# An early order laid out anew, clamps and state transposes on other engines, four sums at the end, and other tile widths in a chunk scan with two feed-forward layers

## The chip, the cores and the metric

One core of a Trainium2 chip runs the whole program. The metric is the device time of one execution in microseconds (us). A core has TensorE (PE in the rows; its weight loads are PEld), VectorE (DVE), ScalarE (ACT), GpSimd (POOL) and SyncE (SP), each with an instruction queue of its own that is worked in order; data comes and goes by DMA transfers that SyncE or ScalarE issue (SPq, ACTq). SBUF is the on-chip memory, PSUM the eight banks into which TensorE writes.

## What is computed

Three layers follow each other. Cut to what matters:

```
x (4, 8, 768, 32)  a (4, 8, 768)  B, C (4, 8, 768, 16)           float32
for each chunk of the sequence, per batch and head:
    L    = exp(cum_i - cum_j) for i >= j      # cum: running sum of log a
    y    = ((C B^T) * L) x + (C state) * exp(cum)
    state = exp(sum log a) * state + sum_j exp(cum_end - cum_j) B_j x_j
X  = y as (3072 tokens, 256)
X1 = (silu(X w_gate) * (X w_val)) w_out       # 256 -> 1536 -> 256
out = relu(X1 w_in)^2 w_out2                  # 256 -> 2048 -> 256
```

The five weights come in double precision (64 bits), x, a, B and C in single precision.

## The kernel before

**Arithmetic.** A wide product is made from three passes of TensorE: each operand is split into a high part (`hi`, `xh_all`) and a low rest (`lo`, `xl_all`), and hi*hi, hi*lo and lo*hi are summed. A pass has 128 rows of weights and up to 512 columns of tokens.

**Weights.** A `Unit` brings two pieces of 512 KB of 64-bit weights into one of two `raw` buffers and turns them into numbers: on ScalarE `share` (L415) and `mag` (L409), the sign on ScalarE (`signs`, L420) or VectorE (`sign`, L424), `clamp` (L430) on VectorE or GpSimd, `shift` (L434) on VectorE; then `split` makes `hi` on ScalarE (L440) and `lo` on GpSimd or VectorE (L444). Nine units hold the first layer: six named gv (gate and value columns for 256 of the 1536 hidden rows, two blocks f of 128) and three named o (the way back). Eight hold the second. `engs` has four digits per unit: sign on ScalarE, clamp on GpSimd, lo on GpSimd, and whether the decode goes in two halves.

**Chunks.** 28 chunks of 112 tokens (96 the last of a batch) carry the scan. For the seven early ones (batch 0) TensorE transposes B and C (`trb`, L497), spreads the decays over the partitions (`ab`, L583) and makes the scores (`cb`, L642); VectorE scans (L592) and multiplies (`times`, L675); TensorE makes the outputs and the state (`ys`, L689); ScalarE keeps the high part (L709) and VectorE the low (L712). The state for the next chunk is turned on VectorE (L724) and put in place by four copies (L729). Later chunks get their transposes by DMA.

**GLU.** Per tile of tokens and block f: six passes for g and six for v (both L737, "front"), silu on ScalarE (L801), the product on VectorE (L804), its high part on ScalarE (L819), its low part p on GpSimd (L824), and six passes back into the sums `acc` (L851). The first 768 tokens form two tiles, 336 and 432 wide, cut into `cells` (pair of blocks, first and last chunk, exact or not) that start as weights and chunks arrive; an exact cell uses single-precision passes on `xf` and needs no splitting. The 2304 tokens after that form five tiles (`tiles`), each with 12 blocks: 60 late steps.

**Second layer.** Six tiles of 512 tokens, 16 blocks each: front L737 (`h`), relu L903, square L906, split L909 and L913, back L923; the last tile's back (L934) has its tokens as rows, 12 passes of 256 columns per block, drained by L982 and L984 and stored.

**Order.** The program is recorded as a graph of operations with costs, priorities and buffers; `Graph.order` plays them through per engine, always the operation with the lowest priority number that is ready, and the list it makes is the order in which each engine runs. The priorities come from the table `PLAN` at the end: `unit_at`, `split_at` and `chunk_at` for weights and early chunks, the order of `cells`, `pace` for late chunks, `second` for the second layer's weights. Where the plan has a gap on TensorE, idle matmuls on zeros (L227, `fills`) are put ahead of the next pass, up to `warm` nanoseconds.

Of the kernel before, what the change touches and what calls it, by code (L numbers as in the profile page):

```python
# [8 lines left out]
F32 = mybir.dt.float32  # L9
# [18 lines left out]
class Op:  # L28
    def __init__(self, eng, cost, fn, deps, prio, bufs, lat):
        self.port = False  # L30
# [5 lines left out]
class Graph:  # L36
# [14 lines left out]
    def order(self):  # L51
# [11 lines left out]
        seq = 0  # L63
        while left:
            started = True
            while started:
                started = False
                for eng, ops in avail.items():
# [20 lines left out]
                    for b in best.bufs:  # L89
                        if not b.taken:  # L90
                            b.taken = True
                            best.after.append(free[b.pool].pop(0))
                    best.start, best.took = now, best.cost
# [13 lines left out]
            while events and events[0][0] <= now:  # L107
                _, _, kind, op = heapq.heappop(events)
                if kind == 0:
                    busy[op.eng] = None  # L110
                    left -= 1
# [18 lines left out]
def kernel(  # L130
# [188 lines left out]
    op_pick = g.add("POOL", 280, setup_pick, prio=-999)  # L319
    op_eye = g.add("POOL", 300, setup_pool, [op_mt], prio=-999.5)  # L320
    op_delta = g.add("POOL", 1200, setup_delta, [op_mt], prio=-999)
    op_mask = g.add("POOL", 950, setup_mask, prio=-997)
# [3 lines left out]
    def dma(eng, n, cost, move, fn, deps=(), prio=0.0, bufs=()):  # L326

        i = g.add(eng, n * cost, fn, deps, prio, bufs, lat=0)
        o = g.add("DMA", move, None, [i], prio, bufs, lat=1700)
        o.issue = i  # L330
# [3 lines left out]
    ld_a = [dma(q, 2, 450, 200, lambda u=u: load_a(u), [], -950) for u, q in enumerate(["SP", "ACT"])]  # L334
    op_clip = g.add("DVE", 900, clip, [*ld_a, op_zero], -950)

    def keep_decays(b):
# [5 lines left out]
        b: dma("SP", 1, 450, 400, lambda b=b: keep_decays(b), [op_clip], 300 + b)  # L343
# [6 lines left out]
    class Unit:  # L350
# [3 lines left out]
        def __init__(self, srcs, prio, after=(), homes=("w", "w"), engs=("DVE", "DVE", False)):  # L354
            raw, self.v, self.hi, self.lo = Buf("raw"), Buf("w"), Buf(homes[0]), Buf(homes[1])
            deps = [
                dma("SP", 1, 450, 1650, lambda s=s, src=src: self.load(raw, s, src), after, prio, [raw])
# [95 lines left out]
    def chunk_ops(k, prio, after=(), load_after=()):  # L453
# [27 lines left out]
        if early:  # L481
# [9 lines left out]
            lb = dma("SP", 1, 480, 650, lambda: load_b(0, B), [op_eb[k % NEB], *load_after], ldp, [e])  # L491
            lc = dma("SP", 1, 480, 650, lambda: load_b(1, C), [op_eb[k % NEB], *load_after], ldp, [e])
# [20 lines left out]
            c.tr = g.add("ACT", 1480, copy_c, [o1, op_mask], prio, [psb, c.bt])  # L513
            c.ebuf = e
        else:
# [10 lines left out]
            lb = c.load = dma("SP", 2, 480, 1300, load_b, [op_bc, *load_after], ldp, [e])  # L526
# [37 lines left out]
            c.tr = dma("SP", 1, 480, 2900, transpose, [o], prio - 3, [bcs, c.bt])  # L564

        lx = dma("SP", 1, 480, 750, load_x, [*load_after, free_x], ldp, [xb])
# [34 lines left out]
        else:  # L601
# [17 lines left out]
            o = dma("SP", 1, 480, 1650, load_ab, [*load_after, kept[b]], ldp, [ab])  # L619
# [532 lines left out]
```

## Time and profile before

| | |
|---|---|
| median of 3 runs | 656.24 us |
| lowest, highest | 656.18, 659.64 us |
| the profiled execution, its own time | 658.71 us |
| span of its records | 656.5 us |
| mean granted TensorE clock in it | 0.987 of full speed |
| TensorE busy | 637.8 us |
| VectorE busy | 393.1 us |
| ScalarE busy | 339.1 us |
| GpSimd busy | 228.5 us |

The rows come from one profiled execution, so sums are set against its span of 656.5 us, with 2.2 us around it. Busy time of TensorE counts every record from start to end; matmuls overlap, and idle matmuls count too, so it is not the same as useful work.

### The profile page before, as it was taken

Reading aid. Unit: us, or ns where it says so; the run is one execution under the profiler, and the core shown is the slowest. Engines: PE = TensorE matmul, PEld = TensorE weight load, DVE = VectorE, ACT = ScalarE, POOL = GpSimd, SP = SyncE. Lnnn points to the kernel's source line nnn. Section 1 sums busy time; section 2 is a strip of 40 time slices with the busy share of each in tenths; the row PEclk is TensorE's granted clock in tenths of the full one; section 3 lists DMA queues with packets and bytes.
Section 4 is the critical chain, followed back from the end, with each engine's and each line's share of the span. In section 5 each row is a group of like instructions: output and inputs, shape, how many; then the busy total and the mean of one; then the engine's idle time right before and its main releaser. Section 6 shows DMA issues by size and latency. Waiting matters only on the chain.

```text
span 656.5 us, 9776 instructions
## 1 busy us (share of the span) xinstructions
PE 637.8 (97%) x3735; PEld 545.7 (83%) x3735; DVE 393.1 (60%) x600; ACT 339.1 (52%) x603; POOL 228.5 (35%) x225
## 2 busy tenths in 40 slices
PE   9899889999999999999999999999999999999997
PEld 7688769888887888878999988888888888888896
DVE  6689575676767647676335755555555555555543
ACT  5579777353435444455446644444444444444442
POOL 6456996654536364534654750000000000000000
PEclk9599999999999999999999999999999999999999
DMA  8488973576455656272322200010010010100100
GB/s 185 102 192 183 182 187 79 108 130 135 88 112 109 117 100 129 55 173 100 108 70 64 65 1 0 1 32 2 0 33 1 0 33 0 33 0 1 33 1 32
DMA packets 153470, 48.89 MB, mean 74 GB/s; under 512 B 141520, under 2 KB 142032, under 8 KB 153424
## 3 DMA queue, kind: packets, MB, share of 16 engines
q1 hardware_dynamic: 152880, 47.92, 34.1%
q8 instruction: 29, 0.48, 0.3%
q10 hardware_dynamic: 544, 0.36, 0.2%
q14 instruction: 17, 0.14, 0.1%
HBM read 34.03 MB, written 3.22 MB: 57 GB/s over the span
## 4 chain that ended last, share of the span: by engine, by line
PE 56%; DVE 1%; POOL 0%; ACT 0%; issue 0%; ACTq 0%
PE h L737 20%; PE acc L923 17%; PE acc L851 5%; PE v L737 5%; PE g L737 5%; PE acc L934 3%; DVE mt L675 0%; DVE L L614 0%; DVE xa L729 0%; PE ys L689 0%; POOL p L824 0%; ACT p L819 0%; DVE xl_all L712 0%; DVE t L804 0%; PE cb L651 0%
## 5 line engine op out<-in xcount | busy, mean ns | idle before, releaser
L824 POOL TENSOR_TENSOR p<-t,p 128x464 fp32r<-128x464 f32 (+3 forms) x84 | 105.4, 1260 | 112.1 <-ACT p L819 112.0
L851 PE MATMUL acc<-p,hi 128*128 128x464 f32 (+4 forms) x336 | 99.9, 374 | 8.2 <-POOL p L824 8.2
L913 DVE TENSOR_TENSOR p<-t,p 128x512 fp32r<-128x512 f32 x96 | 66.3, 690 | 67.9 <-ACT p L909 67.9
L909 ACT ACTIVATE p<-t 128x512 fp32r<-128x512 f32 x96 | 60.8, 633 | 77.9 <-PE acc L923 52.9
L906 DVE TENSOR_TENSOR t<-t 128x512 f32<-128x512 f32 x96 | 66.9, 697 | 53.8 <-ACT t L903 53.8
L923 PE MATMUL acc<-p,hi 128*128 128x512 f32 x320 | 98.5, 389 | 0.0
L804 DVE TENSOR_TENSOR t<-t,v 128x464 f32<-128x464 f32 (+4 forms) x84 | 50.3, 601 | 80.2 <-PE v L737 56.6
L819 ACT ACTIVATE p<-t 128x464 fp32r<-128x464 f32 (+4 forms) x84 | 48.0, 572 | 91.8 <-DVE t L804 83.9
L903 ACT ACTIVATE t<-h 128x512 f32<-128x512 f32 x96 | 57.5, 599 | 63.1 <-PE h L737 62.9
L851 PEld LDWEIGHTS acc<-p,hi 128*128 128x128 f32 x336 | 62.1, 191 | 17.8 <-POOL p L824 12.0
L737 PE MATMUL h<-xh_all,hi 128*128 128x512 f32 x192 | 74.9, 390 | 0.0
L737 PE MATMUL h<-xl_all,hi 128*128 128x512 f32 x192 | 74.9, 390 | 0.0
L737 PE MATMUL h<-xh_all,lo 128*128 128x512 f32 x192 | 74.7, 389 | 0.0
L923 PEld LDWEIGHTS acc<-p,hi 128*128 128x128 f32 x320 | 60.1, 188 | 12.4
L801 ACT ACTIVATE t<-g 128x464 f32<-128x464 f32 (+5 forms) x86 | 44.9, 524 | 42.5 <-PE g L737 39.5
L737 PE MATMUL g<-xh_all,lo 128*128 128x464 f32 (+4 forms) x168 | 60.8, 362 | 1.5 <-POOL lo L444 1.4
L923 PE MATMUL acc<-p,lo 128*128 128x512 f32 x160 | 62.2, 389 | 0.0
L737 PE MATMUL g<-xh_all,hi 128*128 128x464 f32 (+4 forms) x168 | 61.2, 364 | 0.0
L851 PE MATMUL acc<-p,lo 128*128 128x464 f32 (+4 forms) x168 | 61.1, 364 | 0.0
L737 PE MATMUL v<-xh_all,hi 128*128 128x464 f32 (+4 forms) x168 | 60.6, 361 | 0.0
L737 PE MATMUL v<-xh_all,lo 128*128 128x464 f32 (+4 forms) x168 | 60.6, 361 | 0.0
L737 PE MATMUL v<-xl_all,hi 128*128 128x464 f32 (+4 forms) x168 | 60.5, 360 | 0.0
(101 smaller groups left out, 1128.4 us busy)
## 6 DMA issues: line engine op xcount, KB each, us to landing
ab<-decay SPq DMA_DIRECT2D x21, 452.0 KB, 4.0
raw<-in_moe_w_out_dram SPq DMA_DIRECT2D x14, 512.0 KB, 4.7
raw<-in_moe_w_in_dram SPq DMA_DIRECT2D x8, 512.0 KB, 3.9
raw<-in_moe_w_gate_dram SPq DMA_DIRECT2D x6, 512.0 KB, 3.9
raw<-in_moe_w_val_dram SPq DMA_DIRECT2D x6, 512.0 KB, 5.2
xa<-in_x_dram SPq DMA_DIRECT2D x24, 112.0 KB, 2.9
out_dram<-o SPq DMA_DIRECT2D x40, 64.0 KB, 1.9
bc<-in_B_dram SPq DMA_DIRECT2D x18, 56.0 KB, 3.0
```

The lines of the kernel that those rows point to most:

```text
L737: nc.tensor.matmul(ps, l, r, start=(i == 0), stop=(i == len(terms) - 1))
L801: nc.scalar.activation(t[:, :n], gg(), AF.Silu)
L804: nc.vector.tensor_tensor(tb.t[:, :n], tb.t[:, :n], vv(), op=ALU.mult)
L819: nc.scalar.activation(p[:, 0, :n], tb.t[:, :n], AF.Copy)
L824: e.tensor_tensor(p[:, 1, :n], tb.t[:, :n], p[:, 0, :n].bitcast(F32), op=ALU.subtract)
L851: nc.tensor.matmul(ps, l, r, start=bank not in done_f, stop=f == NF - 1, skip_group_check=True,)
L903: nc.scalar.activation(new(tb, [P, TN], F32, "t"), ph.t, AF.Relu)
L906: nc.vector.tensor_tensor(tb.t, tb.t, tb.t, op=ALU.mult)
L909: nc.scalar.activation(new(pb, [P, 2, TN], F32R, "p")[:, 0, :], tb.t, AF.Copy)
L913: e.tensor_tensor(pb.t[:, 1, :], tb.t, pb.t[:, 0, :].bitcast(F32), op=ALU.subtract)
L923: nc.tensor.matmul(acc[-1 - i][m], l.t[:, w], pb.t[:, r, :], start=(f == 0 and s == 0), stop=(f == NF2 - 1 and s == 2),)
L934: nc.tensor.matmul(ps, pb.t[:, l, tk], r, start=(f == 0 and s == 0 and q % 2 == 0), stop=(f == NF2 - 1 and s == 2), skip_group_check=True,)
```

## The change

1. *The planner.* Transfers in the plan are served in the order in which they became ready instead of by priority; no more than 2600 pieces may be queued; several costs are other numbers. These act on the order alone.
2. *The early order.* New numbers for `chunk_at`, `unit_at`, `split_at`, `cells`, `pace` and `second`. The nine units now come as gv2, o1, gv3, o2, gv5, gv4, gv1, gv0, o0. The exact cell is two chunks (224 columns) of unit gv2 instead of one of unit gv4, and a cell of one chunk (112 columns) stands beside it. The second layer's weights are asked for later.
3. *Engines of the decode* (`engs`). No clamp of the first layer is on GpSimd (before: seven of nine units, 12 instructions); signs on ScalarE for seven units (before all nine); lo on GpSimd for four units (before four others) and halves for three (before five): the digits stand in the diff, in the order gv0, o0, gv1, gv2, o1, gv3, gv4, o2, gv5.
4. *Early states.* ScalarE copies the state, TensorE transposes it in two passes (`turn`), ScalarE puts it in place. Late chunks keep VectorE.
5. *Last tile.* Its sums lie in four banks instead of two, and the last block's back is four operations, each with its own drain and store.
6. *Tiles* of 256 and four of 512 tokens instead of three of 464 and two of 456.
7. *`rest`.* The low half of p is made on VectorE in the first 17 late steps, then on GpSimd; in the cells it stays on GpSimd.
8. *Fillers.* Every planned gap of TensorE over 150 ns gets two idle matmuls more than its length gives.

The diff, cut to its core:

```diff
                     for op in ops:
-                        if best is not None and op.prio > best.prio:
+                        if best is not None and (eng == "DMA" or op.prio > best.prio):
+                            continue
+                        if eng != "DMA" and op.pieces and queued + op.pieces > 2600:
                             continue
...
         if not last:
-            st = Buf("st")
+            st, pst = Buf("st"), Buf("ps")
+            to = xa[(k + 1) % NX][0:NS]
+
+            def state():
+                nc.scalar.activation(new(st, [P, HG, NS], F32, "st"), yv()[:, :, Q:P], AF.Copy)
 
             def turn():
-                s = new(st, [P, HG, D], F32, "st")
+                ps = new(pst, [P, 512], F32, "turn")
+                for i in range(HG):
+                    nc.tensor.transpose(ps[0:NS, i * P : (i + 1) * P], st.t[:, i, :], eye)
+
+            def put():
+                nc.scalar.activation(to.rearrange("p h d -> p (h d)"), pst.t[0:NS, 0:256], AF.Copy)
...
-            o = g.add("DVE", 130, turn, [o], prio - 5, [psy, st])
-            ck[k + 1].state = g.add("DVE", 280, put, [o], prio - 5, [st, c.xnext])
+            if early:
+                o = g.add("ACT", 200, state, [o], prio - 5, [psy, st])
+                o = g.add("PE", 200, turn, [o], prio - 5, [st, pst], lat=250)
+                ck[k + 1].state = g.add("ACT", 380, put, [o], prio - 5, [pst, c.xnext])
+            else:
+                o = g.add("DVE", 250, turn_late, [o], prio - 5, [psy, st])
+                ck[k + 1].state = g.add("DVE", 1050, put_late, [o], prio - 5, [st, c.xnext])
...
-            for q in range(4):
-                ps = acc[-1 - i][q // 2][:, q % 2 * 256 : q % 2 * 256 + 256]
+            for q in range(4) if part is None else [part]:
...
                     nc.tensor.matmul(
-                        ps, pb.t[:, l, tk], r,
-                        start=(f == 0 and s == 0 and q % 2 == 0), stop=(f == NF2 - 1 and s == 2),
-                        skip_group_check=True,
+                        acc[-1 - i][q][:, :256], pb.t[:, l, tk], r,
+                        start=(f == 0 and s == 0), stop=(f == NF2 - 1 and s == 2),
                     )
...
+            for q in range(4):
+                ob = Buf("tmp")
+                by_act = q % 2 == 0
...
+                bk = g.add("PE", 3 * 120, lambda q=q: back(q), [o], prio, [ab[q], pb, u.hi, u.lo], lat=260)
+                dr = g.add("ACT" if by_act else "DVE", 390, drain, [bk], prio - GATE, [ab[q], ob])
+                dma("ACT" if by_act else "SP", 1, 480, 500, store, [dr], prio, [ob], 128)
...
-        step_ops.append(glu(tl, f, 0, tl[1] - tl[0], False, 20000 + s * 10, deps)[0])
+        step_ops.append(glu(tl, f, 0, tl[1] - tl[0], False, 20000 + s * 10, deps, s >= PLAN["rest"][1])[0])
...
-                    n = (op.start - free - COLD) / 110 + COLD / 216 if free < 1200 else (op.start - free) / 110
-                    if n >= 1:
-                        fills.append(int(n))
+                    gap = op.start - free
+                    n = (gap - COLD) / 110 + COLD / 216 if free < 1200 else gap / 105
+                    if gap > 150:
+                        fills.append(int(n) + PLAN["more"])
...
 PLAN = dict(
-    chunk_at=[3.5, 20.3, 43.5, 64.7, 45.0, 72.4, 81.6],
+    chunk_at=[40.9, 41.7, 5.7, 61.4, 41.1, 70.4, 58.6],
...
     cells=[
+        (5, 3, 7, 0),
+        (4, 3, 7, 0),
+        (2, 1, 3, 1),
...
-        (4, 3, 4, 1),
-        (4, 4, 7, 0),
...
-    engs=['1101', '1101', '1010', '1111', '1101', '1010', '1100', '1100', '1111'],
-    tiles=[464, 464, 464, 456, 456],
+    engs=['1000', '1000', '1001', '1010', '1001', '1010', '1010', '0011', '0000'],
+    tiles=[256, 512, 512, 512, 512],
     lead=3.5,
     spare=0,
+    more=2,
+    rest=[0, 17],
```

What the new numbers do to the order is seen at two places. The first is TensorE around the first wide GLU pass. In the kernel before, the spread of the fourth chunk (`ab`) is followed by the front of a 336 wide cell:

```order
L583 MATMUL ab<-dv,pick 128x113 x8
L737 MATMUL g<-xh_all,hi 128x336
L737 MATMUL g<-xl_all,hi 128x336
L737 MATMUL g<-xh_all,lo 128x336
L737 MATMUL g<-xh_all,hi 128x336
L737 MATMUL g<-xl_all,hi 128x336
L737 MATMUL g<-xh_all,lo 128x336
L497 MATMUL trb<-eye,eb_101 128x128 x2
```

Now the same place, with the exact cell (`xf`, 224 columns), the seventh chunk's scores (`cb`, 96 columns) and the sixth's outputs (`ys`) and state (`turn`) ahead of it:

```order
L872 MATMUL acc<-t,v 128x224 x2
L647 MATMUL cb<-bct 128x96 x8
L694 MATMUL ys<-mt_108,xa_106 32x128 x8
L758 MATMUL g<-xf,v 128x224 x4
L733 MATMUL turn<-eye,st 16x128 x2
L758 MATMUL g<-xh_all,hi 128x336
L758 MATMUL g<-xl_all,hi 128x336
L758 MATMUL g<-xh_all,lo 128x336
```

The scores of all seven early chunks, and the outputs of six, have moved ahead of the first wide front, where three chunks stood before.

The second place is GpSimd at the change from early to late chunks (`bcs` and `bcr` split B and C for a late chunk, `mt` are its state columns). Before:

```order
L538 TENSOR_TENSOR bcr<-bc_99,bcs 128x256
L444 TENSOR_TENSOR lo<-v,hi 128x1024
L547 TENSOR_TENSOR bcs<-bcr,bcs 128x8x32
L550 TENSOR_TENSOR bcs<-bcr,bcs 128x8x2x16
L430 TENSOR_SCALAR v<-v 128x512 x2
L626 TENSOR_TENSOR mt_108<-bc_99,L 128x8x16
L824 TENSOR_TENSOR p<-t,p 128x336
L626 TENSOR_TENSOR mt_107<-bc_96,L 128x8x16
L430 TENSOR_SCALAR v<-v 128x512
L824 TENSOR_TENSOR p<-t,p 128x336
```

and now:

```order
L543 TENSOR_TENSOR bcr<-bc_99,bcs 128x256
L845 TENSOR_TENSOR p<-t,p 128x336
L552 TENSOR_TENSOR bcs<-bcr,bcs 128x8x32
L555 TENSOR_TENSOR bcs<-bcr,bcs 128x8x2x16
L449 TENSOR_TENSOR lo<-v,hi 128x1024
L631 TENSOR_TENSOR mt_108<-bc_99,L 128x8x16
L631 TENSOR_TENSOR mt_107<-bc_96,L 128x8x16
L845 TENSOR_TENSOR p<-t,p 128x336
L845 TENSOR_TENSOR p<-t,p 128x432 x3
L543 TENSOR_TENSOR bcr<-bc_96,bcs 128x256
```

The clamps (L430) are gone from the queue between the low halves of p, and one low half of weights (`lo`) stands at another place in it.

## Rows read from the trace of the kernel before

**Rows 1.** Stretches: start:end, length, busy (x) of PE, PEld, DVE, ACT, POOL; clock, DMA share, GB/s.

```profile
0.00:34.20 34.20, 30.89 (x278) 23.35 (x278) 21.70 (x47) 20.79 (x34) 19.27 (x36) 0.80 0.65 138
34.20:66.00 31.80, 30.21 (x298) 26.34 (x297) 29.43 (x49) 26.41 (x58) 18.53 (x15) 1.00 0.89 195
66.00:114.70 48.70, 42.18 (x263) 38.51 (x262) 31.33 (x45) 38.32 (x66) 41.75 (x34) 0.96 0.69 150
114.70:652.40 537.70, 534.49 (x2903) 457.48 (x2901) 310.25 (x460) 253.03 (x446) 149.00 (x143) 1.00 0.26 56
```

**Rows 2.** Timeline of TensorE and GpSimd: start us, us, engine, line, out<-in, count.

```profile
33.09 1.15 PE L583 MATMUL ab<-dv,pick 32*128 32x113 f32 x16
34.17 0.42 PE L737 MATMUL g<-xh_all,hi 128*128 128x336 f32 x1
34.43 0.32 PE L737 MATMUL g<-xl_all,hi 128*128 128x336 f32 x1
...
34.89 0.32 PE L737 MATMUL g<-xl_all,hi 128*128 128x336 f32 x1
...
112.19 2.42 POOL L444 TENSOR_TENSOR lo<-v,hi 128x1024 fp32r<-128x1024 f32 x1
...
113.52 0.36 PE L737 MATMUL v<-xh_all,hi 128*128 128x432 f32 x1
...
114.70 0.31 PE L737 MATMUL g<-xh_all,hi 128*128 128x336 f32 x1
...
146.19 0.37 PE L737 MATMUL g<-xh_all,hi 128*128 128x464 f32 x1
146.40 0.38 PE L737 MATMUL g<-xl_all,hi 128*128 128x464 f32 x1
```

**Rows 3.** Chain that ended last, in order of time: start us, us, what, count.

```profile
332.45 1.24 PE g L737 x6
...
396.53 1.36 PE h L737 x6
...
646.61 5.76 PE acc L934 x48
...
652.91 0.38 ACT o L982
```

**Rows 4.** Waits of the whole span: us in total, times, longest us.

```profile
PE acc L851 <- POOL p L824: 8.2, 10, 1.9
```

**Rows 5.** Groups by shape up to 115 us: count, busy us, mean ns, idle before.

```profile
L420 ACT ACTIVATE raw<-raw 128x1024 f16<-128x1024 int32 x4 | 10.0, 2501 | 0.0
L440 ACT ACTIVATE hi<-v 128x1024 fp32r<-128x1024 f32 x9 | 9.6, 1066 | 3.9 <-DVE v L434 3.9
...
L409 ACT ACTIVATE v<-raw 128x1024 f32<-128x1024 f32 x4 | 4.6, 1142 | 0.0
...
L737 PE MATMUL g<-xf,v 128*128 128x112 f32 x16 | 2.4, 283 | 0.0
```

**Rows 6.** Single lines: count, ns min/median/max, first and last start us, shapes.

```profile
L430 POOL TENSOR_SCALAR v<-v x12: 1909/1924/3641, 9.7 to 93.9; 128x512 f32<-128x512 f32 x10, 128x1024 f32<-128x1024 f32 x2
L430 DVE TENSOR_SCALAR v<-v x10: 679/692/1685, 50.1 to 377.3; 128x1024 f32<-128x1024 f32 x10
...
L729 DVE COPY xa<-st x96: 181/186/1182, 13.6 to 297.9; 16x64 f32<-16x64 f32 x96
...
L712 DVE TENSOR_TENSOR xl_all<-ys,xh_all x7: 345/381/392, 15.4 to 63.8; 128x224 fp32r<-128x224 f32 x6, 128x192 fp32r<-128x192 f32 x1
```

**Rows 7.** Timeline of ScalarE at the start: start us, us, engine, line, out<-in.

```profile
5.85 0.28 ACT L501 ACTIVATE bct<-trb 128x128 f32<-128x128 f32 x1 [3.56 <-PE trb L497]
6.02 1.08 ACT L506 ACTIVATE bct<-trb,mask 128x112 f32<-128x112 f32 x4
...
8.36 0.68 ACT L415 ACTIVATE raw<-raw 128x512 int32<-128x512 uint16 x1 [1.26 <-DMA raw<-in_moe_w_gate_dram]
8.93 0.67 ACT L409 ACTIVATE v<-raw 128x512 f32<-128x512 f32 x1
```

More of the change, by code (lines that the diff above doesn't have):

```diff
@@ L29, in __init__ @@
     def __init__(self, eng, cost, fn, deps, prio, bufs, lat):
-        self.port = False
+        self.port, self.pieces = False, 0
         self.eng, self.cost, self.fn, self.prio, self.bufs, self.lat = eng, cost, fn, prio, bufs, lat
@@ L62, in order @@
         left = len(self.ops)
-        seq = 0
+        seq = queued = 0
         while left:
@@ L92, in order @@
                             best.after.append(free[b.pool].pop(0))
+                    queued += best.pieces if eng != "DMA" else 0
                     best.start, best.took = now, best.cost
@@ L110, in order @@
                     busy[op.eng] = None
+                    queued -= op.pieces if op.eng == "DMA" else 0
                     left -= 1
@@ L318, with dma @@
     op_eb = [g.add("POOL", 660, lambda i=i: setup_eb(i), prio=[-1000, -998][i]) for i in range(NEB)]
[L319 to L322, printed above, removed]
+    op_pick = g.add("POOL", 930, setup_pick, prio=-999)
+    op_eye = g.add("POOL", 600, setup_pool, [op_mt], prio=-999.5)
+    op_delta = g.add("POOL", 1940, setup_delta, [op_mt], prio=-999)
+    op_mask = g.add("POOL", 1170, setup_mask, prio=-997)
     op_bc = g.add("POOL", 2200, setup_bc, prio=-900)
     op_tab = g.add("ACT", 1500, act_table, prio=-990)
-    def dma(eng, n, cost, move, fn, deps=(), prio=0.0, bufs=()):
+    def dma(eng, n, cost, move, fn, deps=(), prio=0.0, bufs=(), pieces=256):
         i = g.add(eng, n * cost, fn, deps, prio, bufs, lat=0)
         o = g.add("DMA", move, None, [i], prio, bufs, lat=1700)
+        i.pieces, o.pieces = pieces, pieces
         o.issue = i
@@ L342 @@
     kept = {
-        b: dma("SP", 1, 450, 400, lambda b=b: keep_decays(b), [op_clip], 300 + b)
+        b: dma("SP", 1, 450, 200, lambda b=b: keep_decays(b), [op_clip], 300 + b, pieces=56)
         for b in range(1, NB)
@@ L512, in chunk_ops @@
             o1 = g.add("ACT", 260, copy_b, [o], prio, [psb, c.bt])
-            c.tr = g.add("ACT", 1480, copy_c, [o1, op_mask], prio, [psb, c.bt])
+            c.tr = g.add("ACT", 1080, copy_c, [o1, op_mask], prio, [psb, c.bt])
             c.ebuf = e
@@ L663, in chunk_ops @@
                 o.bufs.append(v)
-            o.cost = 900
+            o.cost = 1140
             o.fn = lambda y=o.fn: (y(), scores_late(0), scores_late(1))
@@ L697, in chunk_ops @@
         dd = slice(b * S + t, b * S + t + n)
-        o = g.add("PE", 620, outputs, [*mults, lx, zs, getattr(c, "state", None)], prio, [xb, c.mt, psy], lat=250)
+        o = g.add("PE", 620 if early else 820, outputs, [*mults, lx, zs, getattr(c, "state", None)], prio, [xb, c.mt, psy], lat=250)
         c.y = o
@@ L913, in rest, with back @@
             e.tensor_tensor(pb.t[:, 1, :], tb.t, pb.t[:, 0, :].bitcast(F32), op=ALU.subtract)
-        def back():
+        def back(part=None):
             if f == 0:
@@ L949, in relu2 @@
         o = g.add("DVE", 690, rest, [o], prio - GATE, [tb, pb], port=True)
-        bk = g.add("PE", 6 * 227 if turned else 12 * 120, back, [o], prio, [*ab, pb, u.hi, u.lo], lat=260)
+        if turned or f < NF2 - 1:
+            bk = g.add("PE", 6 * 227 if turned else 12 * 120, back, [o], prio, [*ab, pb, u.hi, u.lo], lat=260)
         if f == NF2 - 1:
@@ L1024 @@
             deps = [ck[k].xf if exact else ck[k].x for k in range(c0, c1)]
-            glu(tiles[ti], f, o, n, exact, 10000 + i * 10, deps)
+            glu(tiles[ti], f, o, n, exact, 10000 + i * 10, deps, i >= PLAN["rest"][0])
     for ti in range(2):
```

80 lines of the change are left out of this document (34 added, 46 removed).

## The prediction

> **What bounds the kernel now.** The busy times by stretch come first [rows 1]. In the long stretch from 114.7 to 652.4 us TensorE is busy 534.5 of 537.7 us and no other engine passes 58%: there only the work on TensorE counts. In the three stretches ahead of it TensorE looks nearly as full (30.9 of 34.2 us in the first), but much of that is idle matmuls put in to hold the clock, or passes at a low one. So I count useful work: passes by the distance between their starts.
>
> The distances [rows 2, 3]: 0.153 us for 336 columns (34.43 to 34.89, three passes), 0.197 for 432 (113.52 to 114.70, six), 0.21 for 464, 0.207 for 456 (1.24 for six), 0.227 for 512 (1.36 for six), 0.12 for 256 (5.76 for 48); 1.15 for an early chunk's spread or scores. By these and the counts in the code all passes make 609.2 us. The span is 656.5, so 47.3 are lost, in four places:
>
> - ahead of the first wide GLU front, which starts at 34.17: the order has 11.9 us of work there (three chunks and the spread of a fourth), so 22.3 are lost. The mean granted clock is 0.80, so about 40% of the stretch went at the lower level;
> - from there to 114.7, the first use of the last weight unit, whose low half comes from GpSimd's 2.42 us subtraction at 112.19 [rows 2]: 66.5 us of work in 80.5, 14.0 lost. TensorE's back passes wait 8.2 of these for GpSimd's low half of p [rows 4]; a granted clock of 0.96 from 66 on costs another 1.7 or so;
> - the long stretch: 537.7 less 530.8, 6.9 lost;
> - the tail behind the last pass (646.61 + 5.76 = 652.37): 4.1.
>
> ScalarE sums 20.8, 26.4 and 38.3 us in the three early stretches, VectorE 21.7, 29.4, 31.3 and GpSimd 19.3, 18.5, 41.8 [rows 1]: GpSimd is the fullest in the third, just where it is waited for.
>
> **The change part by part.** *Tiles.* Late tokens are 2304 either way. Before: 648 passes at 0.211 and 432 at 0.207, 226.1 us; now 216 at 0.12 and 864 at 0.227, 222.0. That is -4.1 in the stretch where TensorE is full, so it counts whole.
>
> *Cells.* The piece in exact arithmetic grows from 112 to 224 columns, and its cell leaves a narrow piece of 112 behind instead of one of 320. The narrow piece's 36 passes lie between a third and the whole of 0.153 each: 1.8 to 5.5, I take two thirds, 3.6, since overheads do not shrink with columns. They replace 36 at 0.153, -5.5. The old 36 of 320 (336's row in proportion, 5.3) go back to 432 (7.1), +1.8. The exact passes at 112 columns took 2.4 for the front's and about half that again for the back's records [rows 5], 3.6 with overlapping ends; twice as wide they add 0 to 3.6, I take half with the overlap out, 1.9. Together +1.8, bounds -1.9 to +5.4.
>
> *States through TensorE.* Six early chunks lose a VectorE transpose and four copies, 96 copies being the count over all chunks, at a median of 186 ns and at worst 1182 [rows 6]. They gain two small PE transposes: 12 instructions by 0.072 (a spread pass, 1.15 over 16 [rows 2]) is 0.9, bounds 0 and 2; I take 0.7. ScalarE gains two copies per chunk; the nearest row is its 0.28 us copy of 128x128 [rows 7], so 3.4 us in all.
>
> Useful work: 609.2 - 4.1 + 1.8 + 0.7 = 607.6.
>
> *The early order.* This is the large part. All seven early chunks now stand ahead of the first wide front, with the exact cell and the narrow piece: seven spreads, seven scores, 16.1; six outputs and seven transposes, 5.5; the two pieces and the states, 8.3: 29.9 us of work that before lay partly behind it. The question is when that front (call it T0) may start. It needs the hi and lo of the third unit in the new order (the gate and value weights of two row blocks). Ahead of that hi on ScalarE stand three units' decode, each a magnitude of 1.142, a share as long (0.67 and 0.68 at half width [rows 7]) and signs of 2.501 [rows 5], 4.8, so 14.4, with 0.7 for the one in halves; 2.7 of a fourth; three hi copies of 1.07, 3.2; six chunks' mask copies, 0.28 + 1.08 [rows 7], 8.2; x and state copies, about 5. That is 34, or 31 once the starts overlap as they do in the trace (the pass of 0.68 at 8.36 is followed at 8.93). The first pass was at 8.36; the gate weights are now third on SP's queue, so I start at 7.5. At ScalarE's busy share of 34.2 to 66, 26.4 of 31.8 or 0.83 [rows 1], the sum ends at 44.4; the lo on GpSimd (2.4 [rows 2]) and about 2 of queued work give T0 = 49. Bounds: no gaps at all and no queue, 44; the share of the first stretch without its start (20.8 of 28.3, 0.73), 55 to 57. I take 49 because the second stretch, with decode and chunks interleaved, is the nearest row. So the first loss is 49 - 29.9 = 19.1 (14 to 27), before 22.3. The clock matters little here: a low one lengthens passes that wait for ScalarE anyway, and if the added fillers fail to hold it, that is within the upper bound.
>
> *Behind T0.* The work from T0 to the first use of the last unit is 57 us on TensorE. By durations of these rows, the other engines' shares of it are about 46 on ScalarE, 47 on VectorE and 39 on GpSimd, all below TensorE's. GpSimd is rid of 12 clamps (ten at the median of 1.92, two of double width at up to 3.64 [rows 6], some 26 us), which is what its low halves queued behind. I take the 8.2 of waits off, and 1.0 of the 1.7 of low clock: 14.0 becomes 5, bounds 2 (all but the clock) and 14 (nothing gained).
>
> *Clamps on VectorE.* They cost it 0.69 us for 1024 columns (median of ten; at most 1.69 [rows 6]): seven units, 4.8 us, covered as long as VectorE's 47 stay below 57. The spread between 0.69 and 1.69 is the price of colliding with something on GpSimd. Seven at the maximum would add 7 us to 47: 54, still just below 57, but in the chain of weights. The Trainium skill ("SBUF — State Buffer", section on who interferes with whom) says that VectorE and GpSimd share a port pair as an exclusive lock, that a scalar-operand instruction in a two-port mode takes it, and that the other engine then blocks for the whole instruction; it speaks against putting clamps beside GpSimd's subtractions. The maximum of 1.69 against the minimum of 0.68 agrees; by the rule the clamps would rather be priced at 1.7 and the second loss left nearer to 14 than 5, which is the second rival below.
>
> *Rests of p.* The first 17 late steps move their low half to VectorE. In the long stretch it has 227 idle us of 537.7, and TensorE is full: nothing, 0 to 1 off the third loss. That one I take at 6 (4 to 10; fewer, wider tiles mean fewer handovers).
>
> *Weights of the second layer* load later, and transfers go in order of arrival: DMA is a quarter busy in the long stretch [rows 1], so nothing there.
>
> *Last sums in four banks.* Now three drains and stores can begin while the last quarter of the final back runs. The last drain began at 652.91, 0.54 behind the last pass, and took 0.38 [rows 3]; I take 0.5 off 4.1: 3.6 (3.1 to 4.1), for the stores' own landing stays.
>
> The losses: 19.1 + 5 + 6 + 3.6 = 33.7. Span 607.6 + 33.7 = 641.3, 15.2 below 656.5. The profiled execution took 658.71 (2.2 around its span), 2.5 above the median of 656.24; the difference applied to the median gives 641.
>
> **The rivals.**
> *Half of the gain.* The second loss stays at 14, since VectorE's clamps and GpSimd's subtractions get in each other's way in place of GpSimd's clamps: 641 + 9 = 650. T0 at its upper bound of 57 gives 649. For it: the 1.69 us row, and the shares of the first stretch; against it: twelve fewer instructions on the fullest engine.
> *Slower.* Seven chunks ahead of the first front means that the chain from chunk to chunk now sets T0. In the trace the chunks' low halves came from 15.4 to 63.8 [rows 6], 8.1 us each. The chain passes VectorE's in-order queue five times per chunk (two scans, two products, the subtraction), and now decode's clamps stand in that queue. If its pace stays at 8.1, T0 is 15.4 + 6 x 8.1 = 64; the first loss is 34 and, with the second at 14, the time is 641 + 15 + 9 = 665. With the second loss at 14 it is slower by over 0.5% from T0 = 58.5 on (19.1 + 5 + 18.5 = 42.6 of loss in both). Against it: before, PE's wide fronts and the planned order spaced the chunks (useful work lay between them), and 1.2 us of copies per chunk leave VectorE.
> *Better.* No gaps on ScalarE, T0 = 44, and the second loss at 2.5: 641 - 5 - 2.5 = 633.
>
> **How the numbers follow.** Chances: forecast 0.60 (641, itself 636 to 647), half gain 0.24 (650), slower 0.08 (665), better 0.08 (633). The range 632 to 655 takes in the first, the better one and the half gain with some 4 on top for the cells' and the long stretch's upper bounds; the slower case is left out. About 0.5%, or 3.3 us, is what a measurement of this kernel can tell from no change: below 653.0 is faster, above 659.5 slower. Faster gets the forecast, the better case and two thirds of the half gain, 0.84; same the rest of it, 0.08; slower 0.08.
>
> **What would show it.** The first front 336 columns wide should start at 46 to 52 us; at 58 or more the chunk chain or ScalarE held it. The back passes' wait for the low half of p in the early cells should fall from 8.2 to below 3. Clamps on VectorE should keep a median near 0.7; one near 1.7 is the port. The late 512-column passes should start every 0.227, and the long part's end less its useful work should leave 4 to 10. The last store should follow the last pass by 3.1 to 4.1. The prediction is wrong if T0 passes 58, or if the waits for weights (the front on the low half from GpSimd) take over behind T0.

## The result and the profile after

The changed kernel takes 641.93 us (median of four runs, 640.64 to 642.26) where the kernel before takes 657.94 beside it: a ratio of 0.9753, 95% interval 0.9714 to 0.9792. Forecast were 641 us and a range of 632 to 655. The profiled execution took 641.74 us, its span is 640.0. Part of the difference is TensorE's clock. Run again beside the experiments below, the kernel before took 654.3 to 655.0 us where its mean granted clock was 0.997, and 658.6 to 660.2 where it was 0.984; three of the changed kernel's four runs had 0.997 and took 641.7 to 642.3. At the same clock the gain is 12 to 13 us.

The stretches of the changed kernel, cut where its own first wide front starts, where the last weight unit is first used, and where the last pass ends (columns as in [rows 1]):

```profile
0.00:48.28 48.28, 46.04 (x516) 37.77 (x517) 36.59 (x60) 34.18 (x81) 14.61 (x38) 1.00 0.73 166
48.28:112.05 63.77, 59.84 (x386) 56.09 (x383) 51.60 (x64) 49.83 (x81) 49.08 (x35) 0.97 0.72 160
112.05:636.58 524.53, 523.44 (x2867) 437.85 (x2865) 319.58 (x473) 251.08 (x446) 132.29 (x124) 1.00 0.27 57
```

The passes that these cuts come from, in TensorE's timeline, and the end of the chain that ended last (as [rows 2] and [rows 3]):

```profile
48.28 0.40 PE L758 MATMUL g<-xh_all,hi 128*128 128x336 f32 x1
...
64.87 0.65 PE L872 MATMUL acc<-p,hi 128*128 128x336 f32 x1 [2.98 <-POOL p L845]
...
112.05 0.48 PE L872 MATMUL acc<-p,hi 128*128 128x336 f32 x2
...
630.82 5.76 PE acc L953 x48
636.58 0.02 issue
636.60 0.42 DVE o L1000
```

Read as before, by useful work (its amount is the prediction's count, not measured again): up to 48.28 the order has 29.9 us of it, so 18.4 are lost; from there to 112.05 it has 56.9 in 63.8, 6.9 lost; from there to 636.58, 520.8 in 524.5, 3.7 lost; behind the last pass 3.4.

| lost, us | before | forecast | after |
|---|---|---|---|
| ahead of the first wide front | 22.3 | 19.1 | 18.4 |
| from there to the last unit's first use | 14.0 | 5 | 6.9 |
| the long stretch | 6.9 | 6 | 3.7 |
| behind the last pass | 4.1 | 3.6 | 3.4 |
| useful work | 609.2 | 607.6 | 607.6 |

Two more rows say how it came about. TensorE's waits for GpSimd's low half of p, beside [rows 4], and VectorE's clamps, beside [rows 6]:

```profile
PE acc L872 <- POOL p L845: 4.2, 3, 3.0
```

```profile
L435 DVE TENSOR_SCALAR v<-v x20: 409/685/1782, 10.4 to 376.1; 128x1024 f32<-128x1024 f32 x14, 128x512 f32<-128x512 f32 x6
```

The waits have halved, and 3.0 of the 4.2 us are a single one, from 61.9 to 64.87. The clamps kept their median (685 ns, before 692), though six of the twenty are of half width now. The mean granted clock of the first stretch is 1.00, against 0.80.

### The profile page after: what moved, and what is told of

Same layout as the page of the kernel before. It is cut to its first block, busy times and chain, and to the rows that moved or that the text cites. A ratio compares the mean times of both kernels' runs of the same rounds, so it can differ in the third digit from the quotient of the medians.

```text
span 640.0 us, 9839 instructions
## 1 busy us (share of the span) xinstructions
PE 629.3 (98%) x3764; PEld 531.7 (83%) x3764; DVE 408.2 (64%) x598; ACT 335.2 (52%) x607; POOL 196.0 (31%) x196
## 4 chain that ended last, share of the span: by engine, by line
PE 67%; POOL 0%; DVE 0%; ACT 0%; issue 0%; ACTq 0%
PE h L758 20%; PE acc L944 17%; PE acc L872 9%; PE g L758 8%; PE v L758 8%; PE acc L953 4%; PE ys L694 1%; PE cb L656 1%; POOL p L845 0%; ACT p L840 0%; DVE t L825 0%; DVE o L1000 0%; ACTq L840 0%
## 5 line engine op out<-in xcount | busy, mean ns | idle before, releaser
L845 POOL TENSOR_TENSOR p<-t,p 128x512 fp32r<-128x512 f32 (+3 forms) x67 | 91.4, 1368 | 102.4 <-ACT p L840 100.9
L872 PE MATMUL acc<-p,hi 128*128 128x512 f32 (+4 forms) x336 | 95.6, 367 | 4.3 <-POOL p L845 4.2
L840 ACT ACTIVATE p<-t 128x512 fp32r<-128x512 f32 (+4 forms) x84 | 47.5, 565 | 73.9 <-DVE t L825 70.5
L825 DVE TENSOR_TENSOR t<-t,v 128x512 f32<-128x512 f32 (+2 forms) x70 | 44.8, 641 | 63.0 <-PE v L758 49.0
L822 ACT ACTIVATE t<-g 128x512 f32<-128x512 f32 (+5 forms) x86 | 45.0, 523 | 51.9 <-PE g L758 51.3
L872 PEld LDWEIGHTS acc<-p,hi 128*128 128x128 f32 x336 | 59.9, 190 | 13.1 <-POOL p L845 5.7
L758 PE MATMUL g<-xh_all,hi 128*128 128x512 f32 (+4 forms) x196 | 69.0, 352 | 0.0
L758 PE MATMUL g<-xl_all,hi 128*128 128x512 f32 (+4 forms) x196 | 68.3, 348 | 0.0
L758 PE MATMUL g<-xh_all,lo 128*128 128x512 f32 (+4 forms) x196 | 68.3, 348 | 0.0
L872 PE MATMUL acc<-p,lo 128*128 128x512 f32 (+4 forms) x168 | 60.6, 361 | 0.0
L758 PE MATMUL v<-xh_all,hi 128*128 128x512 f32 (+2 forms) x140 | 52.4, 374 | 0.7 <-DVE xl_all L717 0.7
L758 PE MATMUL v<-xl_all,hi 128*128 128x512 f32 (+2 forms) x140 | 52.3, 373 | 0.0
```

Of the source, the lines that this page charges most:

```text
L758: nc.tensor.matmul(ps, l, r, start=(i == 0), stop=(i == len(terms) - 1))
L822: nc.scalar.activation(t[:, :n], gg(), AF.Silu)
L825: nc.vector.tensor_tensor(tb.t[:, :n], tb.t[:, :n], vv(), op=ALU.mult)
L840: nc.scalar.activation(p[:, 0, :n], tb.t[:, :n], AF.Copy)
L845: e.tensor_tensor(p[:, 1, :n], tb.t[:, :n], p[:, 0, :n].bitcast(F32), op=ALU.subtract)
L872: nc.tensor.matmul(ps, l, r, start=bank not in done_f, stop=f == NF - 1, skip_group_check=True,)
```

## The experiments

All edit the changed kernel; the time to compare is 641.9 us, with its first wide front at 48.28. Where an edit swaps an engine "in its own order", the planned order stays as it was, so that nothing but the engine differs. The changed kernel was not run again beside them, and for differences under 2 us the spread of the runs decides. The stretches shown are of one profiled execution each.

| kernel | median, lowest to highest, us | first wide front |
|---|---|---|
| old tiles | 645.8, 645.2 to 646.4 | 48.0 |
| clamps on GpSimd | 649.0, 648.8 to 651.4 | 50.2 |
| early states on VectorE | 644.9, 642.2 to 646.3 | 52.8 |
| fewer idle matmuls | 640.2, 639.5 to 641.5 | 47.8 |
| old tables | 651.7, 650.6 to 652.2 | 32.6 |
| magnitudes twice | 646.8, 646.1 to 648.1 | 52.9 |
| low halves twice | 641.2, 640.2 to 642.6 | 48.7 |
| rests on GpSimd | 642.6, 641.9 to 643.6 | 48.6 |
| one low half on VectorE | 640.1, 639.9 to 640.3 | 48.3 |
| first chunk first | 642.7, 640.8 to 646.9 | 47.7 |
| last two and fewer idle matmuls | 642.2, 639.6 to 643.3 | 48.2 |
| two banks | 642.2, 641.0 to 644.3 | 48.9 |

**The tiles.**

```diff
-    tiles=[256, 512, 512, 512, 512],
+    tiles=[464, 464, 464, 456, 456],
```

> The changed kernel with its late tiles again 464, 464, 464, 456, 456 wide; nothing else. Theory (a term of useful work alone): the 1080 passes take 226.1 us instead of 222.0, so the time is 641.9 + 4.1 = 646 (645 to 647), and the first 336 wide front and the first late front stay where they are within 0.5 us. Rival (the width also pays in handovers, since the loss in the long stretch fell from 6.9 to about 3.7): 4.1 + 3 = 649.

645.8: 3.9 us, near the 4.1 of useful work. The front stands at 48.0. In its profiled run the last pass ends 3.1 us later, and the span ends 4.2 us behind it instead of 3.4, so not all of the 3.9 is passes; but no other loss is added, and the smaller loss in the long stretch is not the width's.

**The clamps.** The seven units that had them on GpSimd before get them back, each at its place in the order.

```diff
         def clamp(self, e, c):
             v = self.part(c)
+            if self in [W1[u] for u, d in zip(units, "110110111") if d == "1"]:
+                e = "POOL"
```

> The changed kernel in its own order, but the clamps of the seven first-layer units that had them on GpSimd before are issued on GpSimd again, each at its place in the order: about 26 us more on GpSimd by the rows of before. Theory (GpSimd's queue is what low halves of p and of the weights wait behind): the loss behind the first wide front goes from 6.9 back to 12 to 16, the time to 648 to 653; the first wide front moves by at most 3 us. Rival (clamps on VectorE lose as much to collisions with GpSimd as they win): 640 to 643.

649.0, 7.1 more, as the theory had it. Where, GpSimd's timeline of that kernel shows, and TensorE's behind it:

```profile
57.86 4.15 POOL L451 TENSOR_TENSOR lo<-v,hi 128x1024 fp32r<-128x1024 f32 x1
61.97 1.83 POOL L633 TENSOR_TENSOR mt<-bc,L 128x128 f32<-128x128 f32 x2
63.76 3.62 POOL L437 TENSOR_SCALAR v<-v 128x1024 f32<-128x1024 f32 x1
67.35 2.94 POOL L847 TENSOR_TENSOR p<-t,p 128x336 fp32r<-128x336 f32 x2
```

```profile
68.30 0.65 PE L874 MATMUL acc<-p,hi 128*128 128x336 f32 x1 [4.50 <-POOL p L847]
```

A clamp of 3.62 us is in front of the p that TensorE needs. But waits of this kind sum to only 6.3 in the whole run, 2.1 above the changed kernel. Set against the same passes there, TensorE is 1.9 us late at the first wide front (it waits 0.8 for GpSimd's state columns at 17.1, and the clock is low behind that), 4.5 at 73.9, behind that wait, and 9.6 from 126.5 on. The last part is another wait: a clamp that GpSimd makes at 112.35 holds the last unit's shift on VectorE, its hi on ScalarE and so TensorE:

```profile
112.35 3.62 POOL L437 TENSOR_SCALAR v<-v 128x1024 f32<-128x1024 f32 x1
```

```profile
116.00 1.93 DVE L441 SCALAR_TENSOR_TENSOR v<-v,raw 128x1024 uint32<-128x1024 uint32 x1 [3.29 <-POOL v L437]
```

```profile
119.07 0.57 PE L874 MATMUL acc<-p,hi 128*128 128x336 f32 x2 [0.75 <-ACT hi L447]
```

The clock falls around both waits:

```profile
63.00:72.00 9.00, 4.50 (x16) 4.01 (x15) 2.58 (x3) 5.33 (x5) 9.00 (x7) 0.71 0.85 152
...
112.00:130.00 18.00, 16.57 (x106) 15.17 (x105) 11.78 (x18) 7.87 (x18) 11.43 (x10) 0.91 0.55 111
```

The clock is not the main cost: the profiled execution, at a mean clock of 0.989, was the slowest of the four (651.4), and the other three took 648.8 to 649.2 at 0.995 to 0.997, the changed kernel's own level. So about 7 us remain without any difference in the clock.

**The early states.** VectorE turns and places them as before, in the changed kernel's order.

```diff
             def state():
-                nc.scalar.activation(new(st, [P, HG, NS], F32, "st"), yv()[:, :, Q:P], AF.Copy)
+                turn_late()
 
             def turn():
-                ps = new(pst, [P, 512], F32, "turn")
-                for i in range(HG):
-                    nc.tensor.transpose(ps[0:NS, i * P : (i + 1) * P], st.t[:, i, :], eye)
+                put_late()
 
             def put():
-                nc.scalar.activation(to.rearrange("p h d -> p (h d)"), pst.t[0:NS, 0:256], AF.Copy)
+                pass
```

> The changed kernel in its own order, but the six early states are turned and placed on VectorE as before (a transpose and four copies, 1.4 us each time, 8.4 in all) where ScalarE and TensorE had them; ScalarE is rid of 0.56 us six times, 3.4. Theory (ScalarE's sum sets the first wide front, at 48.3): the front at 45 to 48.5, time 639 to 642. Rival (the chain from chunk to chunk through VectorE sets it): six times 0.6 to 1.4 us later, front at 52 to 56, time 645 to 650.

The front moves to 52.8, the rival's value, but not by the rival's six equal steps. TensorE at three places of this kernel; the changed one reaches the first two at 23.91 and 44.03:

```profile
22.40 0.30 PE L756 MATMUL g<-xh_all,hi 128*128 128x112 f32 x1
...
45.61 1.86 PE L870 MATMUL acc<-t,v 128*128 128x224 f32 x4
...
52.83 0.47 PE L756 MATMUL g<-xh_all,hi 128*128 128x336 f32 x1
```

Up to 24 the theory holds: with less on ScalarE, TensorE is 1.5 us ahead. Then VectorE takes it back. The transposes took 1.5 us and the copies 6.2 there, 7.7 in all, and VectorE is full from 24 to 48 (23.5 of 24 us). The stretches 24 to 48 and 48 to the front of this kernel:

```profile
24.00:48.00 24.00, 22.24 (x258) 17.96 (x257) 23.50 (x52) 15.48 (x43) 5.12 (x8) 0.95 0.64 143
48.00:52.80 4.80, 4.80 (x37) 4.03 (x36) 3.17 (x10) 1.38 (x2) 0.00 (x0) 0.54 0.76 153
```

and the same first stretch of the changed kernel, with VectorE at 21.7 and TensorE never idle:

```profile
24.00:48.00 24.00, 24.00 (x307) 20.28 (x306) 21.70 (x36) 16.72 (x54) 5.04 (x8) 1.00 0.70 153
```

TensorE stood for 1.8 of the 24 us: near 26 for GpSimd's state columns, which had waited for VectorE's scans, and near 43 for the scans themselves. At 45.61 it is 1.6 us late. The other 3.0 of the 4.6 us are the clock: from there to the front the same passes took 7.2 us instead of 4.2, at 0.54 from 48 on. The time, 644.9, lies 3.0 above the changed kernel and just under the rival's range. The fastest of the four runs, 642.2 at a mean clock of 0.999, is within the changed kernel's spread; the others, 644.0 to 646.3, had 0.992 to 0.995. So most of the 3.0 goes with the clock.

**Idle matmuls by the old rule.**

```diff
-                    gap = op.start - free
-                    n = (gap - COLD) / 110 + COLD / 216 if free < 1200 else gap / 105
-                    if gap > 150:
-                        fills.append(int(n) + PLAN["more"])
+                    n = (op.start - free - COLD) / 110 + COLD / 216 if free < 1200 else (op.start - free) / 110
+                    if n >= 1:
+                        fills.append(int(n))
```

> The changed kernel with the idle matmuls counted by the old rule (none in gaps under 110 ns, no two extra, 110 instead of 105 ns each); same order of everything else. Theory (in the first stretch TensorE waits for ScalarE, so a lower clock costs little): mean granted clock of the first 48 us falls from 1.00 to 0.8 to 0.95, first wide front later by 0 to 2, time 642 to 644. Rival (the clock is what the first stretch gained by): front later by 4 to 6, time 646 to 648.

Neither: 98 instead of 114 are recorded, the clock of the first 48 us stays at 1.00, the front comes at 47.8, and the time is 640.2. The additional ones bring nothing here (the ranges, 639.5 to 641.5 and 640.6 to 642.3, overlap). What a low clock in the first stretch costs was not seen in this run, since the clock did not fall.

**The old tables.** The tables `chunk_at`, `unit_at`, `split_at`, `cells`, `pace`, `second` and `engs` of the kernel before in the changed code; two lines of it:

```diff
-    engs=['1000', '1000', '1001', '1010', '1001', '1010', '1010', '0011', '0000'],
+    engs=['1101', '1101', '1010', '1111', '1101', '1010', '1100', '1100', '1111'],
...
-    pace=[-124, 0.68, 119],
+    pace=[-43, 2.78, 32],
```

> The changed kernel's code, tiles, rests, fillers and last tile, with the tables of the early order (chunks, units, splits, cells, pace, second layer's weights) and the digits for the decode's engines of the kernel before. Theory (the early order with its engines brought the part of the gain that the tiles did not): losses of 22.3 and 14.0 again in place of 18.4 and 6.9, less 1.1 of useful work: 641.9 + 10 = 652 (649 to 655). Rival (new code, fillers and states through TensorE brought it whatever the tables): 641 to 646.

651.7, 9.7 above the changed kernel, with the front back at 32.6. The kernel before took 655.1 beside it, 3.4 more, about the tiles' 3.9; the 9.7 and the 3.9 make 13.6, near the 12 to 13 us at the same clock. The edit takes back the order and the engines together; since the clamps alone cost 7.1 in the new order, the runs do not tell the two apart. The clock of its first 48 us is 1.00, as it is in the new order with the old rule for idle matmuls; so which part of the change lifts it from 0.80 is not shown.

**What sets the first front.** Two edits, one for ScalarE, one for VectorE.

```diff
-            nc.scalar.activation(self.part(c), self.words(raw, c)[1].bitcast(F32), AF.Abs, scale=65536.0)
+            for _ in range(2 if self in W1.values() else 1):
+                nc.scalar.activation(self.part(c), self.words(raw, c)[1].bitcast(F32), AF.Abs, scale=65536.0)
```

> The changed kernel with each magnitude pass of the nine first-layer units issued twice on ScalarE (the second writes the same numbers): two of 1.12 and four of 0.67 us, 4.9 us more ahead of the hi that the first wide front needs. Theory (ScalarE's sum sets that front): front later by 4 to 6, at 52 to 54, time 646 to 649. Rival (the chunk chain through VectorE sets it): front later by 0 to 2, time 642 to 644.

The front at 52.9 and the time at 646.8: 4.6 and 4.9 later, for 4.9 us on ScalarE. But not each of the 4.9 us counts:

```profile
22.70 0.39 PE L734 MATMUL turn<-eye,st 128*16 128x128 f32 x2 [1.98 <-ACT st L729]
...
28.51 0.30 PE L759 MATMUL g<-xh_all,hi 128*128 128x112 f32 x1
```

In the changed kernel these two start at 19.65 and 23.91: TensorE is 3.1 us late, then 4.6, and stays so up to the front, although the last 1.3 us of added magnitudes come only at 38 to 42. Between 24 and 29 its granted clock was 0.66, which may be part of the 4.6.

```diff
         def keep_l():
-            nc.vector.tensor_tensor(
-                xl_all[:, :, dd], yv()[:, :, :n], xh_all[:, :, dd].bitcast(F32), op=ALU.subtract
-            )
+            for _ in range(2 if early else 1):
+                nc.vector.tensor_tensor(
+                    xl_all[:, :, dd], yv()[:, :, :n], xh_all[:, :, dd].bitcast(F32), op=ALU.subtract
+                )
```

> The changed kernel with the low half of the seven early chunks' outputs made twice on VectorE: 0.39 us each, 2.3 us ahead of the first wide front. Theory (ScalarE's sum sets the front): later by 0 to 1, time 641 to 643. Rival (the chunk chain through VectorE): later by 2.0 to 2.7, time 644 to 645.

The front at 48.7, 641.2: VectorE has room for 2.3 us, but, by the states above, not for 7.7.

**Rests on GpSimd.**

```diff
-    rest=[0, 17],
+    rest=[0, 0],
```

> The changed kernel with all low halves of p on GpSimd, the first 17 late steps too. Theory (the long stretch is full of passes on TensorE and hides it): within 1 us of 641.9. Rival (GpSimd, still busy with late chunks, holds back passes there): 644 to 648, with the waits of the back passes for GpSimd above 6 us.

642.6, the waits 4.6: 0.7 us, inside the spread, as the theory had it.

**The stall at 61.9.** GpSimd's and VectorE's timelines of the changed kernel there:

```profile
53.57 2.41 POOL L552 TENSOR_TENSOR bcs<-bcr,bcs 128x256 bf16<-128x256 f32 x1
55.94 2.41 POOL L555 TENSOR_TENSOR bcs<-bcr,bcs 128x256 bf16<-128x256 f32 x1
58.32 2.93 POOL L449 TENSOR_TENSOR lo<-v,hi 128x1024 fp32r<-128x1024 f32 x1
61.21 1.39 POOL L631 TENSOR_TENSOR mt<-bc,L 128x128 f32<-128x128 f32 x1
```

```profile
53.02 2.48 DVE L619 TENSOR_TENSOR_SCAN L<-ab,delta 128x904 f32<-128x904 f32 x1
55.43 0.47 DVE L825 TENSOR_TENSOR t<-t,v 128x336 f32<-128x336 f32 x1
55.83 2.06 DVE L619 TENSOR_TENSOR_SCAN L<-ab,delta 128x904 f32<-128x904 f32 x1
```

The two splits have a median of 0.68 us; begun during a scan, each takes 2.41. The edit moves one low half of p from behind them to VectorE:

```diff
-                e = nc.gpsimd if pool_rest else nc.vector
+                e = nc.gpsimd if pool_rest and not (tl == tiles[0] and f == 7) else nc.vector
```

> The changed kernel in its own order with one instruction on another engine: the low half of p of block 7 of the first 336 wide cell is made on VectorE, at its place in the order, instead of GpSimd. In the trace the back passes stood 3.1 us at 61.6 for it, since GpSimd did two splits of B and C (2.41 us each beside VectorE's scans, 0.68 at other times) and a low half of weights (2.93) ahead of it. Theory (that queue is the stall): the gap at 61 falls below 1 us, the low clock of 65 to 68 goes, time 637 to 640. Rival (the pass waits for something else as well, or the wait moves to the next back): 641 to 643.

The gap at 61 is gone, and the low clock behind it. The stretch 61 to 70 of the changed kernel and of this one:

```profile
61.00:70.00 9.00, 6.02 (x25) 5.50 (x24) 4.33 (x4) 6.65 (x8) 6.40 (x6) 0.81 1.07 234
```

```profile
61.00:70.00 9.00, 8.17 (x46) 6.73 (x46) 7.89 (x9) 8.18 (x10) 6.89 (x6) 1.00 1.10 232
```

The time is 640.1, 1.8 less and 0.1 above the theory's range. Part of the wait came back: 1.35 us at 77.6, and two shorter ones. TensorE, 4.2 us ahead of the changed kernel's passes at 64.0, is only 1.8 ahead from 78.7 on, and 1.7 is what the low clock cost there (0.19 of 9 us). Nor does the clock fall behind every such wait. The same pass with its wait, and the stretch 61 to 70, in the kernel with fewer idle matmuls and in that with the old tiles:

```profile
64.02 0.42 PE L872 MATMUL acc<-p,hi 128*128 128x336 f32 x1 [2.61 <-POOL p L845]
```

```profile
61.00:70.00 9.00, 6.39 (x40) 5.72 (x39) 5.63 (x7) 6.59 (x9) 7.17 (x6) 1.00 1.01 237
```

```profile
64.07 0.65 PE L872 MATMUL acc<-p,hi 128*128 128x336 f32 x1 [2.45 <-POOL p L845]
```

```profile
61.00:70.00 9.00, 6.55 (x30) 5.82 (x29) 4.23 (x5) 6.61 (x9) 5.75 (x6) 0.81 0.98 239
```

The first of these two keeps the wait and took 640.2, as little as the kernel without it. The one of the changed kernel's four runs with a mean clock of 1.000 took 640.6. So the 1.8 us are about what the low clock costs; that the wait by itself costs anything on balance is not shown.

On VectorE the moved subtraction took long itself, since GpSimd was in its low half of weights, from 58.61 on:

```profile
59.20 2.72 DVE L845 TENSOR_TENSOR p<-t,p 128x336 fp32r<-128x336 f32 x1
```

**The first chunk first.** TensorE loses most of its 18 us before 24. In the changed kernel ScalarE does 4.3 us of decode ahead of the first chunk's copies:

```profile
8.22 1.14 ACT L420 ACTIVATE raw<-raw 128x1024 int32<-128x1024 uint16 x1 [5.91 <-DMA raw<-in_moe_w_val_dram]
9.25 1.11 ACT L414 ACTIVATE v<-raw 128x1024 f32<-128x1024 f32 x1
10.26 2.47 ACT L425 ACTIVATE raw<-raw 128x1024 f16<-128x1024 int32 x1
12.48 0.36 ACT L506 ACTIVATE bct<-trb 128x128 f32<-128x128 f32 x1
```

The edit puts the first chunk's loads, transposes, copies, spread and scans in front (`c.first` collects them), with 21 idle matmuls ahead of its transposes:

```diff
+    head = [op_mt, *op_eb, op_pick, op_eye, op_delta, op_mask, op_tab, op_zero, *[d.issue for d in ld_a], op_clip, *ck[0].first, *ck[0].scans[0].deps, *ck[0].scans]
+    order.sort(key=lambda op: op not in head)
```

> The changed kernel with the first chunk's B and C loaded ahead of the first weights, and its transposes, ScalarE copies, spread and scans issued ahead of the first unit's decode (21 idle matmuls ahead of its transposes instead of the planned number); all else in its order. TensorE loses 18 of its first 24 us, and in the trace the first scores start at 13.1, behind 4.3 us of decode on ScalarE. Theory (ScalarE is full from 8.2 to 36, so only the 1.3 us of copies that go into its idle time are won): first scores at 8, first wide front at 46 to 48, time 640 to 641. Rival (the chain from chunk to chunk paces the first stretch): front at 43 to 45, time 637 to 639.

The first scores start at 8.8 instead of 13.1, 4.3 us earlier, and the first wide front at 47.7, 0.6 earlier: the theory's value. TensorE waited 1.2 us for the second chunk's B and C, the decode now starts at 8.81 instead of 8.22, and by 19.05 the head start is down to 0.6: ScalarE's queue took the rest of it back. The median of 642.7 (640.8 to 646.9) shows no gain; the slowest of the four had a mean clock of 0.987.

**Together.** The edits of the last two kernels and the old rule for idle matmuls; the changed lines are those of the three diffs above.

> The two edits of the runs beside it together with the older rule for idle matmuls (the run with it alone took 640.2). If the two gains add: 636 to 639. If the stall at 61 or the first stretch only shifts its loss: 640 to 642.

642.2 (639.6 to 643.3): the gains did not add, and no version here is clearly better than the changed kernel beyond the 1.8 us of the single edits.

**The last sums.** The function `relu2` of the kernel before in place of the new one; its core:

```diff
-            accbuf[-1 - i] = [Buf("ps") for _ in range(2 if turned else 4)]
+            accbuf[-1 - i] = [Buf("ps") for _ in range(2)]
...
-        if turned or f < NF2 - 1:
-            bk = g.add("PE", 6 * 227 if turned else 12 * 120, back, [o], prio, [*ab, pb, u.hi, u.lo], lat=260)
+        bk = g.add("PE", 6 * 227 if turned else 12 * 120, back, [o], prio, [*ab, pb, u.hi, u.lo], lat=260)
```

> The changed kernel with the last tile's sums in two banks, one last back and two drains per bank, as before. Theory: the time from the last pass to the end of the span goes from 3.4 back to 4.1, and the time by as much: 642 to 643. Rival (the first drains were never what ended last): 641.9, tail 3.4 to 3.6.

The chain of this kernel ends with two drains one behind the other again:

```profile
632.72 5.76 PE acc L955 x48
638.49 0.02 issue
638.51 0.43 DVE o L1005
...
639.03 0.38 ACT o L1003
```

From 638.48 to the span's end at 642.5 are 4.0 us, against 3.4; the time, 642.2, cannot tell 0.6 from nothing. Nor can the tail: with four banks it was 4.2 in the kernel with the old tiles and 3.8 in that with the old tables. What the four banks bring is not shown.

## Why the prediction was right, and where its steps were not

*Useful work.* The tiles' -4.1 is measured as 3.9. The 607.6 in all is not measured by itself: the losses are counted against it, and none came out below nothing. No run tries the cells' 1.8 or the states' 0.7 alone.

*The first front at 49.* Right by number (48.28), but by errors that cancel, so with luck. The first decode began at 8.22, not 7.5, and the sum's own terms (31 at a share of 0.83) end at 44.8, not 44.4. ScalarE was fuller than the 0.83 taken from the stretch before: from 8.22 to 36 it stands idle for under 1 us, and the third unit's hi was done at 41.4, not 44.4, its lo at 43.8, not 47. And the 2 us of work queued behind that were 4.5. TensorE's last idle matmuls ahead of the front ran at 30.17; from there on it worked without a gap through the chunks in its order, and reached the front when it was done with them:

```profile
30.17 0.94 PE L231 MATMUL trb<-idle 128*128 128x256 bf16 x7
30.94 0.38 PE L502 MATMUL trb<-eye,eb 128*128 128x128 f32 x2
...
46.52 1.78 PE L758 MATMUL g<-xf,v 128*128 128x224 f32 x8
48.14 0.38 PE L733 MATMUL turn<-eye,st 128*16 128x128 f32 x2
```

So ScalarE sets the pace of the first 30 us (magnitudes twice: the whole 4.6 us are there by 28.5; states on VectorE: 1.5 us won by 24; first chunk first: of 4.3 us almost nothing is left), and TensorE's own chunk work the rest. That is also why "the clock matters little here" was wrong as argued: behind 30 us a low clock delays the front, as the states on VectorE showed with 7.2 us for passes of 4.2. And the kernel before itself takes some 5 us longer at 0.984 than at 0.997.

*The states.* The step priced them by TensorE's passes alone, 0.7 us, with ScalarE's copies; that VectorE's relief was worth anything stood only in the slower rival. It is worth 3 us in the median: without it the front is at 52.8, 1.6 us by VectorE's queue and 3.0 by the clock that fell behind it. The rival's mechanism (the chunk chain through VectorE) is thus real, though not at its price, and the change itself is what keeps it from setting the front; VectorE has 2.3 us of room, and not 7.7.

*Behind the front.* The second loss was forecast at 5 and is 6.9, but the step had its cause only in part. It took 8.2 us of waits for p off this stretch, where [rows 4] is a sum over the whole span. The same row up to 114.7 in the kernel before, and up to 112.05 in the changed one:

```profile
PE acc L851 <- POOL p L824: 5.1, 5, 1.9
```

```profile
PE acc L872 <- POOL p L845: 3.2, 2, 3.0
```

So 1.9 of the 7.1 us that the loss fell by are these waits. All idle time of TensorE in the stretch fell by 4.2 (80.5 less 72.4 busy [rows 1], to 63.77 less 59.84); the other 2.9 are passes that follow each other at other distances than counted, and why stays open. The 1.0 of low clock did not come: it cost 1.7 again, behind the one wait of 3.0, and that is what one edit won back. That the clamps matter is shown: put back, they cost 7.1 us. But they do so by the weights of the last unit and by the first front as well as by the waits for p. That 5 came near 6.9 is in part luck. The half-gain rival, in which VectorE and GpSimd block each other, has its mechanism in the rows (1.78 us for a clamp, 2.41 for a split begun during a scan) but not its price: the median clamp stayed at 685 ns.

*The long stretch* lost 3.7 instead of 6, just under its bounds of 4 to 10; the tiles are not the reason, nor is the low half of p on VectorE in 17 steps (0.7 us, inside the spread). What else it was has not been tried.

*The tail* is 3.4 for 3.6.

## What to carry to other kernels

Cost a new order by stretches with useful work against time, and ask of each stretch which queue has no gap: here it was ScalarE for 30 us and then TensorE itself, and one sum over ScalarE gave the right number for a partly wrong reason. When an operation moves off an engine, price the engine it leaves as well as the one it goes to: the states' move looked like a cost of 0.7 us and was worth 3. Read a wait in the stretch that you price, not over the whole span. And look at the clock around each wait of a full TensorE: at the same pass it fell to 0.81 over 9 us behind waits of 3.0 and 2.5 us, and stayed at 1.00 behind one of 2.6. Its price there was 1.7 us, so kernels are best compared at the same mean clock.

## What the runs showed of the hardware

A VectorE instruction with two operands in SBUF and a GpSimd instruction held each other up, and the one that began later took longer. Six of GpSimd's 42 splits began during a scan and took 2.41 to 2.48 us, where the median is 0.68; one that began at 103.41, 0.04 ahead of a scan, took 0.68, and the scan 2.53, where the scans' median is 2.04. VectorE's subtraction for 336 columns, begun 0.6 us into a GpSimd subtraction of 2.94, took 2.72 us; for 512 columns with GpSimd idle it took 0.68. The Trainium skill ("SBUF — State Buffer", section on who interferes with whom) says that a VectorE instruction with two SBUF inputs contends with a GpSimd instruction that reads SBUF; these rows agree. What the forecast had weighed, clamps in a two-port mode, is the smaller part of it here: their maximum is 1.78 us (for one begun during GpSimd's low half of p), and the median did not move.
